# Decayed linear attention and token mixer on one core: decay moved to v and q, heads as array tiles, states by one scan, casts on GpSimd, mixer in four stages

## The chip, the cores and the metric

The kernel runs on one core of one Trainium2 chip. The metric is the device time of one execution in microseconds; before the change three runs gave 182.01 us as the median (181.44 to 183.78). Engines: PE is TensorE (matmul and transpose), DVE is VectorE, ACT is ScalarE, POOL is GpSimd, SP is SyncE, which here only issues transfers. Each engine runs its own instructions in the order in which they stand and waits for others by semaphores.

## The reference

Inputs: q, k, v of shape (4 batches, 8 heads, 768 tokens, 64), one decay lam per head, three weights. Cut to what matters:

```python
for b in range(nb):                                   # blocks of 64 tokens
    intra = einsum('bhic,bhjc->bhij', qb, kb) * Dmask # lam ** (i - j), lower triangle
    intra = einsum('bhij,bhjd->bhid', intra, vb)
    inter = einsum('bhid,bhde->bhie', qb * lam_pow, kv_state)
    out[:, :, sl] = intra + inter
    kv_state = lam_block * kv_state + einsum('bhsd,bhse->bhde', kb * rev_pow, vb)
x = out as (batch, token, 512)
wq, wk = x @ w_q, x @ w_k                             # 64 columns each
mixed = (wq @ wk.T / 8) @ x                           # over all tokens of a batch
result = relu(mixed) @ w_out
```

Both kernels use chunks of 128 tokens, write lam ** (i - j) as lam ** (i + 1) on the query side times lam ** -(j + 1) on the key side (counted from the start of the sequence), and compute mixed as wq (wk.T x), with Y = wk.T x.

## The kernel before, in words

A **pair** is two neighbouring heads of one batch (128 columns together); there are four pairs in a batch and 16 in all. The kernel goes through them in groups of two (`attention_pair`, L193), and after each second group comes the mixer of that batch (`hypermixer`, L296).

Set-up builds, for each pair number, three decay tables with Exp on ACT: dqT (lam ** t, transposed layout), dkT (not read later) and dkn (lam ** -t, natural layout), L131 to L142, and four padded query tiles `qTpad`, whose other half is zero (L62). `issue_dma` (L171) loads q and k from SP's queue and v from ACT's, one transfer of 192 KB for each head, one group ahead.

For each pair: ACT casts q (L199) and v (L201) to bf16, POOL multiplies k by dkn into khn (L203). PE transposes both (L208, L210); DVE multiplies the transposed q by dqT into two padded tiles (L212, L215), ACT copies the transposed k (L219). Then for each of six chunks: PE computes scores of both heads with all 128 rows of the array (L234; the zeros of qTpad take out the other head), DVE masks them (L242), PE multiplies with v into one half of the columns each (`ops`, L250), adds the state's part (L258), and forms this chunk's contribution to the state (`dps`, L268), which DVE adds to the running state gsb (L279). Every three chunks ACT copies `ops` into xT (L283).

The mixer of a batch: PE transposes xT back in 24 pieces (xnp, L302; DVE copies to xnat, L307), then wq (L313; ACT), wk (24 small matmuls, L326; DVE), Y (L338; DVE), `pm` (L351; ACT with relu into rmT) and the output product `po` (24 matmuls of 512 columns, L364; DVE copies to osb, L372; SP writes it out). All PSUM tiles rotate through one pool of eight banks, and osb through two buffers.

The program is written with a tile framework: a scheduler orders each engine's instructions from the dependencies, buffers and the order in which the code is written.

Of the kernel before, what the change touches and what calls it, by code (L numbers as in the profile page):

```python
# [10 lines left out]
BF16 = mybir.dt.bfloat16  # L12
# [5 lines left out]
BLK = 64  # L18
NB = S // BLK
# [10 lines left out]
def kernel(  # L30
# [14 lines left out]
    stage = ctx.enter_context(tc.tile_pool(name="stage", bufs=4))  # L45
    sbf = ctx.enter_context(tc.tile_pool(name="sbf", bufs=3))
    tsb = ctx.enter_context(tc.tile_pool(name="tsb", bufs=3))
    smk = ctx.enter_context(tc.tile_pool(name="smk", bufs=4))
    gsbp = ctx.enter_context(tc.tile_pool(name="gsb", bufs=4))
    xtp = ctx.enter_context(tc.tile_pool(name="xt", bufs=2))  # L50
    hyp = ctx.enter_context(tc.tile_pool(name="hyp", bufs=1))
    outp = ctx.enter_context(tc.tile_pool(name="outp", bufs=2))
    ps1 = ctx.enter_context(tc.tile_pool(name="ps1", bufs=8, space=bass.MemoryType.PSUM))
# [3 lines left out]
    qTpad = []  # L57
    for s_slot in range(2):
        pair = []
        for hl in range(2):  # L60
            qt = consts.tile([128, S], BF16, name=f"qTpad{s_slot}{hl}")
            nc.gpsimd.memset(qt[(1 - hl) * 64 : (1 - hl) * 64 + 64, :], 0.0)  # L62
            pair.append(qt)
        qTpad.append(pair)

    iota_i = consts.tile([128, 2, CH], F32, name="iota_i")
    nc.gpsimd.iota(
        iota_i,
        pattern=[[0, 2], [1, CH]],
        base=0,  # L70
        channel_multiplier=0,
        allow_small_or_imprecise_dtypes=True,
    )
    iota_p = consts.tile([128, 1], F32, name="iota_p")
    nc.gpsimd.iota(
        iota_p,
        pattern=[[0, 1]],
        base=0,
        channel_multiplier=1,
        allow_small_or_imprecise_dtypes=True,  # L80
    )
# [20 lines left out]
    EN4 = consts.tile([128, NCH, 2, D], F32, name="EN4")  # L102
    nc.gpsimd.iota(
        EN4,
        pattern=[[128, NCH], [0, 2], [0, D]],
# [3 lines left out]
    )  # L109

    lam_all = consts.tile([128, H], F32, name="lam_all")
    nc.sync.dma_start(out=lam_all, in_=lam.partition_broadcast(128))
    lnlam_all = consts.tile([128, H], F32, name="lnlam_all")
    nc.scalar.activation(out=lnlam_all, in_=lam_all, func=ACT.Ln)
    nlnlam_all = consts.tile([128, H], F32, name="nlnlam_all")
    nc.vector.tensor_scalar_mul(out=nlnlam_all, in0=lnlam_all, scalar1=-1.0)

    DqT = []
    DkT = []
    Dkn = []  # L120
    for kk in range(H // 2):
        lncol = consts.tile([128, 1], F32, name=f"lncol{kk}")
        nc.vector.tensor_copy(out=lncol[0:64, 0:1], in_=lnlam_all[0:64, 2 * kk : 2 * kk + 1])
        nc.vector.tensor_copy(
            out=lncol[64:128, 0:1], in_=lnlam_all[64:128, 2 * kk + 1 : 2 * kk + 2]
        )
        nlncol = consts.tile([128, 1], F32, name=f"nlncol{kk}")
        nc.vector.tensor_scalar_mul(out=nlncol, in0=lncol, scalar1=-1.0)
# [31 lines left out]
    def slot_col(hl, m, a):  # L160
        return (hl * 3 + (m - 6 * a) // 2) * BLK
# [261 lines left out]
```

## Time and profile before

| | |
|---|---|
| three runs, median | 182.01 us |
| span of the profiled execution | 179.5 us |
| PE busy | 120.8 us in 1272 matmuls |
| DVE busy | 98.8 us in 282 instructions |
| ACT busy | 79.0 us in 139 |
| POOL busy | 31.5 us in 30 |
| mean granted clock of PE | 0.903 of full speed |
| DMA | 26.7 MB, mean 149 GB/s |

A busy PE is not a PE at its peak: matmuls overlap, so a matmul's own time (about 0.26 us for 128 columns) is much longer than the distance to the next one. Times of a stage are therefore read from starts. [...]

### The profile page before, as it was taken

How to read it: one execution, taken by the hardware profiler on the slowest of the kernel's cores; microseconds unless marked ns; L12 is line 12 of the kernel's file. 1: busy time of each engine (PE TensorE's matmuls, PEld its weight loads, DVE VectorE, ACT ScalarE, POOL GpSimd, SP SyncE). 2: the span in 40 equal slices, each digit the busy share in tenths (PEclk: the TensorE clock that was granted, in tenths of full speed). 3: DMA queues.
4: the chain of work that ended last, by engine and by line, in shares of the span. 5: the costliest groups of instructions: out<-in, count | busy, mean ns of one | idle time of the engine just before them, and what ended most of it. 6: DMA issues, size and time to landing. Idle time of an engine off the chain costs nothing.

```text
span 179.5 us, 3380 instructions
## 1 busy us (share of the span) xinstructions
PE 120.8 (67%) x1272; PEld 73.6 (41%) x1272; DVE 98.8 (55%) x282; ACT 79.0 (44%) x139; POOL 31.5 (18%) x30
## 2 busy tenths in 40 slices
PE   0000038959969749779969679599697596896930
PEld 0000025636533426556534457375334374663310
DVE  0630018879532488677322896785327876972232
ACT  3019994665628501651534603926254016131600
POOL 8402520331600000606100005115000030000000
PEclk9999999999999985885899956969999759999995
DMA  3999949999997985497943650610005300000063
GB/s 84 328 285 282 270 108 262 285 260 240 237 225 158 295 243 167 102 257 172 219 91 104 201 177 4 147 28 4 0 4 220 128 4 2 4 0 4 0 234 117
DMA packets 80464, 26.70 MB, mean 149 GB/s; under 512 B 76864, under 2 KB 76864, under 8 KB 80448
## 3 DMA queue, kind: packets, MB, share of 16 engines
q1 hardware_dynamic: 55360, 20.20, 42.7%
q10 hardware_dynamic: 25088, 6.29, 15.5%
q8 instruction: 10, 0.16, 0.4%
q14 instruction: 6, 0.05, 0.1%
HBM read 20.19 MB, written 6.29 MB: 148 GB/s over the span
## 4 chain that ended last, share of the span: by engine, by line
PE 42%; issue 17%; DVE 14%; DMA 12%; ACT 11%; POOL 1%; ACTq 0%; DVEq 0%; POOLq 0%
PE po L364 7%; PE ops L250 7%; PE spsum L234 6%; DVE smask L242 5%; DMA out_dram<-osb 4%; PE xnp L302 4%; DMA vf<-in_v_dram 4%; DVE osb L372 3%; PE trq L208 3%; PE pq L313 3%; PE py L338 3%; PE pm L351 2%; PE ops L258 2%; ACT dkn L137 2%; DMA lam_all<-in_lam_dram 2%
## 5 line engine op out<-in xcount | busy, mean ns | idle before, releaser
L203 POOL TENSOR_TENSOR khn<-kf,dkn 128x768 bf16<-128x768 f32 x16 | 26.0, 1642 | 115.9 <-issue 78.2
L242 DVE TENSOR_TENSOR smask<-spsum,maskc 128x256 bf16<-128x256 f32 x96 | 36.5, 415 | 3.8 <-PE spsum L234 2.7
L234 PE MATMUL spsum<-qTpad,khatT 128*128 128x128 bf16 x192 | 25.6, 257 | 14.6 <-ACT khatT L219 7.5
L250 PE MATMUL ops<-smask,vn 128*64 128x128 bf16 x192 | 25.9, 265 | 5.5 <-DVE smask L242 5.2
L283 ACT CAST xT<-ops 128x384 bf16<-128x384 f32 x32 | 14.2, 481 | 34.7 <-PE ops L258 31.4
L372 DVE COPY osb<-po 128x512 f32<-128x512 f32 x24 | 16.0, 687 | 22.6 <-PE po L364 15.4
L208 PE MATMUL trq<-ident,qn 128*128 128x128 bf16 x96 | 11.2, 240 | 25.5 <-ACT qn L199 25.5
L364 PE MATMUL po<-wo_sb,rmT 128*128 128x512 bf16 x96 | 22.2, 380 | 0.0
L234 PEld LDWEIGHTS <-khatT 128*128 128x128 bf16 x192 | 13.5, 110 | 19.4 <-ACT khatT L219 13.8
L250 PEld LDWEIGHTS <-vn 128*64 128x64 bf16 x192 | 15.6, 121 | 14.1 <-issue 10.2
L212 DVE TENSOR_TENSOR qTpad<-trq,dqT 64x768 bf16<-64x768 bf16 x16 | 8.8, 549 | 22.5 <-PE trq L208 17.8
L258 PE MATMUL ops<-qTpad,gsb 128*64 128x128 bf16 x160 | 21.2, 260 | 0.0
L199 ACT CAST qn<-qf 128x768 bf16<-128x768 f32 x16 | 13.4, 838 | 15.1 <-PE trq L208 15.1
L358 ACT ACTIVATE rmT<-pm 128x512 bf16<-128x512 f32 (+1 forms) x32 | 12.7, 518 | 13.4 <-PE pm L351 13.4
L208 PEld LDWEIGHTS <-qn 128*128 128x128 bf16 x96 | 6.8, 106 | 28.2 <-ACT qn L199 25.8
L201 ACT CAST vn<-vf 128x768 bf16<-128x768 f32 x16 | 13.5, 842 | 8.1 <-PE ops L258 7.3
L268 PE MATMUL dps<-vn,khn 128*64 128x64 bf16 x160 | 16.6, 223 | 0.0
L219 ACT COPY khatT<-trk 128x768 bf16<-128x768 bf16 x16 | 12.5, 803 | 3.2 <-PE trk L210 3.1
L364 PEld LDWEIGHTS <-rmT 128*128 128x128 bf16 x96 | 8.2, 98 | 13.3 <-ACT rmT L358 5.7
L307 DVE COPY xnat<-xnp 128x512 bf16<-128x512 bf16 x24 | 8.9, 417 | 8.3 <-PE xnp L302 8.2
L279 DVE TENSOR_TENSOR gsb<-dps,gsb 128x64 bf16<-128x64 f32 x64 | 11.8, 215 | 2.4 <-PE dps L268 1.3
L258 PEld LDWEIGHTS <-gsb 128*64 128x64 bf16 x160 | 11.6, 129 | 2.7 <-issue 1.6
(44 smaller groups left out, 122.0 us busy)
## 6 DMA issues: line engine op xcount, KB each, us to landing
vf<-in_v_dram ACTq DMA_DIRECT2D x32, 192.0 KB, 4.4
qf<-in_q_dram SPq DMA_DIRECT2D x32, 192.0 KB, 4.0
kf<-in_k_dram SPq DMA_DIRECT2D x32, 192.0 KB, 3.9
out_dram<-osb SPq DMA_DIRECT2D x24, 256.0 KB, 2.1
wo_f<-in_moe_w_out_dram SPq DMA_DIRECT2D x1, 1024.0 KB, 7.2
wq_f<-in_moe_w_q_dram SPq DMA_DIRECT2D x1, 128.0 KB, 4.2
wk_f<-in_moe_w_k_dram SPq DMA_DIRECT2D x1, 128.0 KB, 4.9
lam_all<-in_lam_dram SPq DMA_DIRECT2D x1, 4.0 KB, 3.5
```

Of the source, the lines that this page charges most:

```text
L199: nc.scalar.copy(out=qn, in_=st.qf)
L201: nc.scalar.copy(out=vn, in_=st.vf)
L203: nc.gpsimd.tensor_tensor(out=khn, in0=st.kf, in1=Dkn[kk], op=ALU.mult)
L208: nc.tensor.transpose(trq[:, c * CH : (c + 1) * CH], qn[:, c, :, :], ident)
L234: nc.tensor.matmul(spsum[:, hl * CH : (hl + 1) * CH], L["khatT"][:, c * CH : (c + 1) * CH], L["qt"][hl][:, c * CH : (c + 1) * CH], start=True,
L242: nc.vector.tensor_tensor(out=smask, in0=spsum, in1=maskc, op=ALU.mult)
L250: nc.tensor.matmul(oreg, L["vn"][:, c, hl, :], Hh["smask"][:, hl * CH : (hl + 1) * CH], start=True, stop=(c == 0),)
L258: nc.tensor.matmul(oreg, gsb[:, :], L["qt"][hl][:, c * CH : (c + 1) * CH], start=False, stop=True,)
L268: nc.tensor.matmul(dps[hl * 64 : hl * 64 + 64, :], L["khn"][:, c, hl, :], L["vn"][:, c, hl, :], start=True, stop=True,)
L283: nc.scalar.copy(out=xT[st.b][:, st.kk, a * HALF : (a + 1) * HALF], in_=Hh["ops"],)
L364: nc.tensor.matmul(po, rmT[:, kt, stt * 128 : (stt + 1) * 128], wo_sb[:, kt, :], start=(kt == 0), stop=(kt == 3),)
L372: nc.vector.tensor_copy(out=osb, in_=po)
```

## The change

The attention part and the mixer are rewritten; loads, pools and order follow.

- **Loads**: one transfer of 384 KB for both heads of a pair, q, k and v all from SP's queue, two pairs ahead in the code, nine buffers for each; the weights come after pair 3.
- **Decay**: only on v (a small table DvI, 128 x 48, spread by broadcast) and on the transposed q (four tables Dq). k stays as it is.
- **Casts**: q and k are cast, and v is multiplied and cast, on POOL.
- **Heads as array tiles**: scores of a head use its 64 rows only (kT and qT slices at rows 0 or 64), with no padded tiles. The state's part uses 64 rows and 64 columns.
- **States by one scan**: all five chunk contributions of a pair are put into one PSUM tile, and one DVE scan with coefficients 0 and 1 makes the running sums for all chunks.
- **Masks** work on three chunks of a head at a time (128 x 384).
- **flip**: the transposes of xT back are done pair by pair, into one bank.
- **Mixer**: q and k projections in one matmul; wk by six transposes from that; Y and osb copied by ACT; a generator in four stages, of which one is run beside each pair of the next batch; the last batch's runs at the end.

```diff
-            nc.scalar.dma_start(
-                out=st.vf[:, :, hl, :],
+    def load(b, kk):
+        st = {}
+        for nm, src in (("q", q), ("k", k), ("v", v)):
+            t = stage.tile([128, 2, NCH, D], F32, tag="f" + nm, name="f" + nm)
+            nc.sync.dma_start(
+                out=t,
+                in_=src[b, 2 * kk : 2 * kk + 2].rearrange("h (c p) d -> p h c d", p=128),
+            )
...
+    staged = {0: load(*pairs[0]), 1: load(*pairs[1])}
...
-        dq = consts.tile([128, S], BF16, name=f"dqT{kk}")
-        nc.scalar.activation(out=dq, in_=ET, func=ACT.Exp, scale=lncol)
-        dk = consts.tile([128, S], BF16, name=f"dkT{kk}")
-        nc.scalar.activation(out=dk, in_=ET, func=ACT.Exp, scale=nlncol)
-        dkn = consts.tile([128, NCH, 2, D], BF16, name=f"dkn{kk}")
+    nc.scalar.preload_act_table_set("natural_log_exp_and_others")
...
+    DvI = consts.tile([128, H, NCH], F32, name="DvI")
+    nc.scalar.activation(out=DvI, in_=pw48, func=ACT.Exp, scale=-1.0)
...
+        nc.scalar.activation(out=t, in_=ET, func=ACT.Exp, scale=lncol[:, kk : kk + 1])
...
+    def prepare(n):
...
+        nc.gpsimd.tensor_copy(out=qn, in_=f["q"].rearrange("p h c d -> p c h d"))
+        kn = nat.tile([128, NCH, 2, D], BF16, tag="kn", name="kn")
+        nc.gpsimd.tensor_copy(out=kn, in_=f["k"].rearrange("p h c d -> p c h d"))
+        vn = nat.tile([128, 2, NCH, D], BF16, tag="vn", name="vn")
+        nc.gpsimd.tensor_tensor(
+            out=vn,
+            in0=f["v"],
+            in1=DvI[:, 2 * kk : 2 * kk + 2, :].unsqueeze(3).to_broadcast([128, 2, NCH, D]),
...
+            nc.tensor.transpose(trq[:, c * CH : (c + 1) * CH], qn[:, c, :, :], ident)
+        qT = tsb.tile([128, S], BF16, tag="qT", name="qT")
+        nc.vector.tensor_tensor(out=qT, in0=trq, in1=Dq[kk], op=ALU.mult)
...
+        nc.scalar.copy(out=kT, in_=trk)
+
+        dps = pst([128, D, NCH - 1], F32, "dps")
+        for c in range(NCH - 1):
+            for hl in range(2):
+                nc.tensor.matmul(
+                    dps[hl * 64 : hl * 64 + 64, :, c],
+                    kn[:, c, hl, :],
+                    vn[:, hl, c, :],
...
+        nc.vector.tensor_tensor_scan(
+            out=gs.rearrange("p e c -> p (e c)"),
+            data0=coef.rearrange("p e c -> p (e c)"),
+            data1=dps.rearrange("p e c -> p (e c)"),
...
+    def attend(n, L):
...
         for a in range(2):
...
+            sc = [pst([128, 3, CH], F32, f"sc{hl}") for hl in range(2)]
...
+                    r = slice(hl * 64, hl * 64 + 64)
+                    nc.tensor.matmul(
+                        sc[hl][:, cc, :],
+                        kT[r, c * CH : (c + 1) * CH],
+                        qT[r, c * CH : (c + 1) * CH],
...
+                    nc.tensor.matmul(
+                        oa[r, cc, :],
+                        gs[r, :, c - 1],
+                        qT[r, c * CH : (c + 1) * CH],
...
+                nc.vector.tensor_tensor(out=t, in0=sc[hl], in1=maskc, op=ALU.mult)
...
+                    nc.tensor.matmul(
+                        oa[r, cc, :],
+                        vn[:, hl, c, :],
+                        pr[hl][:, cc, :],
...
+            nc.scalar.copy(out=xT[b][:, kk, a * HALF : (a + 1) * HALF], in_=oa)
+
+    def flip(n):
...
+            nc.tensor.transpose(xp[:, t, :], xT[b][:, kk, t * CH : (t + 1) * CH], ident)
+        nc.vector.tensor_copy(out=xnat[b][:, :, kk * CH : (kk + 1) * CH], in_=xp)
...
+    def mixer(b):
...
+            nc.scalar.copy(out=qkT[:, n * HALF : (n + 1) * HALF], in_=pq)
...
+            nc.tensor.transpose(
+                pk[:, t, :], qkT[64:128, t * CH : (t + 1) * CH], ident[64:128, 64:128]
+            )
...
+        nc.scalar.copy(out=Y, in_=py)
+        yield
...
+        yield
...
+            nc.scalar.copy(out=osb, in_=po)
+            nc.sync.dma_start(out=out[b, t * CH : (t + 1) * CH, :], in_=osb)
+            if t % 3 == 2:
+                yield
...
+    ready = {0: prepare(0)}
+    mix = None
+    for n in range(N):
+        if n + 2 < N:
+            staged[n + 2] = load(*pairs[n + 2])
+        if n == 1:
+            load_weights()
+        if n + 1 < N:
+            ready[n + 1] = prepare(n + 1)
+        attend(n, ready.pop(n))
+        if n % NP == 0 and n > 0:
+            mix = mixer(n // NP - 1)
+        if mix is not None:
+            next(mix, None)
+        flip(n)
```

How the order of the instructions moves is seen at three places. The first is the start of the program on ACT. Before, with vf the v loads, dqT, dkT and dkn the tables:

```order
L186 DMA vf<-in_v_dram 128x6x64 x2
L114 ACT_TABLE_LOAD
L114 ACTIVATE lnlam_all<-lam_all 128x8 [waits DMAHW1_49]
L186 DMA vf<-in_v_dram 128x6x64 x3
L186 DMA vf<-in_v_dram 128x6x64 [waits DMAHW3_49]
L186 DMA vf<-in_v_dram 128x6x64 [waits DMAHW5_49]
L186 DMA vf<-in_v_dram 128x6x64 [waits DMAHW7_49]
L131 ACT_TABLE_LOAD [waits DVE_49]
L131 ACTIVATE dqT_121<-ET,lncol_116 128x768 [waits Pool_49]
L133 ACTIVATE dkT_123<-ET,nlncol_119 128x768 [waits DVE_49]
L137 ACTIVATE dkn_125<-EN_108,nlnlam_all 128x6x64 [waits Pool_49]
```

After:

```order
L105 ACT_TABLE_LOAD
L107 ACTIVATE lnl<-lam_all 128x8 [waits DMAHW0_49]
L126 ACTIVATE dq_124<-ET,lncol 128x768 [waits DVE_49,Pool_49]
L122 ACTIVATE DvI<-pw_120 128x48 [waits DVE_49]
L126 ACTIVATE dq_126<-ET,lncol 128x768
L126 ACTIVATE dq_128<-ET,lncol 128x768
L126 ACTIVATE dq_130<-ET,lncol 128x768
L176 COPY kT<-trk 128x768 [waits PE_49] x2
```

The six later v loads, of which three wait for a transfer, and the second table load are gone from between lnl and the first table; four tables and DvI stand ahead of the first copy of a transposed k.

The second place is DVE in the attention of the second batch. Before, a part of two pairs' chunks (smask the masked scores, gsb the running state, osb the output of the mixer before):

```order
L242 TENSOR_TENSOR smask_882<-spsum_879,maskc_104 128x256
L242 TENSOR_TENSOR smask_887<-spsum_884,maskc_104 128x256
L277 CAST gsb_894<-dps_891 128x64
L277 CAST gsb_901<-dps_898 128x64
L372 COPY osb_799<-po_794 128x512
L372 COPY osb_807<-po_802 128x512
L242 TENSOR_TENSOR smask_906<-spsum_903,maskc_104 128x256
L242 TENSOR_TENSOR smask_911<-spsum_908,maskc_104 128x256
L279 TENSOR_TENSOR gsb_920<-dps_917,gsb_894 128x64
L279 TENSOR_TENSOR gsb_929<-dps_926,gsb_901 128x64
```

After, one whole pair, beside the mixer's third or fourth stage (qT the decayed queries, gs all running states, pr the masked scores of a head's three chunks, xnat the flipped xT):

```order
L171 TENSOR_TENSOR qT_989<-trq_982,dq0_124 128x768
L190 SCALAR_TENSOR_TENSOR gs_1011<-coef_111,dps_1000 128x320
L240 TENSOR_TENSOR pr_1026<-sc0_1013,maskc_108 128x384
L240 TENSOR_TENSOR pr_1028<-sc1_1014,maskc_108 128x384
L240 TENSOR_TENSOR pr_1052<-sc0_1037,maskc_108 128x384
L240 TENSOR_TENSOR pr_1054<-sc1_1038,maskc_108 128x384
L261 COPY xnat_629<-xp_1087 128x6x128
```

A pair has seven DVE instructions, none of them the mixer's, where two pairs' chunks and osb copies alternated.

The third place is ACT beside the mixer's second stage. Before, after the mixer's relu (rmT) come the casts of the next pairs:

```order
L358 ACTIVATE rmT_737<-pm_753 128x256
L358 ACTIVATE rmT_737<-pm_756 128x512
L358 ACTIVATE rmT_737<-pm_759 128x256
L199 CAST qn_1057<-qf_811 128x768
L201 CAST vn_1059<-vf_813 128x768
L186 DMA vf_1429<-in_v_dram 128x6x64 x2
```

After, the eight rmT alternate with a pair's kT and xT:

```order
L176 COPY kT_747<-trk_740 128x768
L305 ACTIVATE rmT_812<-pm_813 128x384
L305 ACTIVATE rmT_812<-pm_816 128x384
L254 CAST xT_628<-oa_770 128x384
L305 ACTIVATE rmT_812<-pm_819 128x384
L305 ACTIVATE rmT_812<-pm_822 128x384
L254 CAST xT_628<-oa_794 128x384
L305 ACTIVATE rmT_812<-pm_825 128x384
L305 ACTIVATE rmT_812<-pm_828 128x384
L305 ACTIVATE rmT_812<-pm_831 128x384
L305 ACTIVATE rmT_812<-pm_834 128x384
L176 COPY kT_873<-trk_866 128x768
```

The relu of a batch now stands between the copies of the next batch's second pair; the last four come before the next kT.

## Rows read from the trace of the kernel before

**Rows 1.** The page: busy time (share, instructions); clock and GB/s by fortieths.

```profile
PE 120.8 (67%) x1272; PEld 73.6 (41%) x1272; DVE 98.8 (55%) x282; ACT 79.0 (44%) x139; POOL 31.5 (18%) x30
...
PEclk9999999999999985885899956969999759999995
...
GB/s 84 328 285 282 270 108 262 285 260 240 237 225 158 295 243 167 102 257 172 219 91 104 201 177 4 147 28 4 0 4 220 128 4 2 4 0 4 0 234 117
```

**Rows 2.** The chain that ended last, in order of time: start us, us, what.

```profile
4.66 7.47 DMA vf<-in_v_dram
...
25.49 0.82 PE trq L208 x6
...
44.79 0.33 PE xnp L302 x4
...
157.30 0.33 PE xnp L302 x4
...
175.25 0.69 DVE osb L372
```

**Rows 3.** PE in order of time: start us, us, line, tile, array shape, count.

```profile
40.40 0.40 PE L234 MATMUL spsum<-qTpad,khatT 128*128 128x128 bf16 x4
40.73 0.25 PE L268 MATMUL dps<-vn,khn 128*64 128x64 bf16 x4
40.91 0.40 PE L234 MATMUL spsum<-qTpad,khatT 128*128 128x128 bf16 x4
41.24 0.25 PE L250 MATMUL ops<-smask,vn 128*64 128x128 bf16 x2
...
41.53 0.25 PE L250 MATMUL ops<-smask,vn 128*64 128x128 bf16 x2
...
45.28 0.68 PE L302 MATMUL xnp<-ident,xT 128*128 128x128 bf16 x9
45.89 0.25 PE L250 MATMUL ops<-smask,vn 128*64 128x128 bf16 x2
...
50.58 1.48 PE L338 MATMUL py<-xnat,wkn 128*64 128x512 bf16 x6 [0.65 <-DVE wkn L333]
...
84.19 1.14 PE L302 MATMUL xnp<-ident,xT 128*128 128x128 bf16 x9
...
130.56 5.60 PE L364 MATMUL po<-wo_sb,rmT 128*128 128x512 bf16 x24
```

**Rows 4.** Groups by shape: line, engine, tile, count, busy us, mean ns, idle before.

```profile
L242 DVE TENSOR_TENSOR smask<-spsum,maskc 128x256 bf16<-128x256 f32 x96 | 36.5, 415 | 3.8 <-PE spsum L234 2.7
L203 POOL TENSOR_TENSOR khn<-kf,dkn 128x768 bf16<-128x768 f32 x16 | 26.0, 1642 | 115.9 <-issue 78.2 <-PE dps L268 17.3 <-ACT dkn L137 12.6
...
L283 ACT CAST xT<-ops 128x384 bf16<-128x384 f32 x32 | 14.2, 481 | 34.7 <-PE ops L258 31.4 <-DMA vf<-in_v_dram 3.1
...
L219 ACT COPY khatT<-trk 128x768 bf16<-128x768 bf16 x16 | 12.5, 803 | 3.2 <-PE trk L210 3.1
L279 DVE TENSOR_TENSOR gsb<-dps,gsb 128x64 bf16<-128x64 f32 x64 | 11.8, 215 | 2.4 <-PE dps L268 1.3
...
L358 ACT ACTIVATE rmT<-pm 128x512 bf16<-128x512 f32 x16 | 9.9, 620 | 13.4 <-PE pm L351 13.4
L215 DVE TENSOR_TENSOR qTpad<-trq,dqT 64x768 bf16<-64x768 bf16 x16 | 9.0, 561 | 0.5
L307 DVE COPY xnat<-xnp 128x512 bf16<-128x512 bf16 x24 | 8.9, 417 | 8.3 <-PE xnp L302 8.2
...
L95 POOL IOTA ET<- 128x768 f32 x1 | 0.8, 764 | 0.0
```

**Rows 5.** One stretch: us, busy time (count) of each engine, granted clock, DMA share, GB/s.

```profile
60.00:85.00 25.00, 18.43 (x226) 13.05 (x224) 19.51 (x58) 10.06 (x16) 5.69 (x4) 0.76 0.81 203
```

More of the change, by code (lines that the diff above doesn't have):

```diff
@@ L55 @@
+    pairs = [(b, kk) for b in range(B) for kk in range(NP)]
+    lam_all = consts.tile([128, H], F32, name="lam_all")
+    nc.sync.dma_start(out=lam_all, in_=lam.partition_broadcast(128))
+    staged = {0: load(*pairs[0]), 1: load(*pairs[1])}
     ident = consts.tile([128, 128], BF16, name="ident")
     make_identity(nc, ident)
[L57 to L64, printed above, removed]
@@ L109 @@
     )
[L111 to L123, printed above, removed]
+    maskc = consts.tile([128, 3, CH], BF16, name="maskc")
@@ L222, in attention_pair @@
+    def attend(n, L):
+        b, kk = pairs[n]
+        if b not in xT:
+            xT[b] = xtp.tile([128, NP, S], BF16, tag="xT", name="xT")
+            xnat[b] = xtp.tile([128, NCH, HD], BF16, tag="xnat", name="xnat")
+        qT, kT, vn, gs = L["qT"], L["kT"], L["vn"], L["gs"]
         for a in range(2):
-            half = {}
-            for st in streams:
-                ops = ps1.tile([128, HALF], F32, tag="p1", name="ops")
-                half[id(st)] = dict(ops=ops)
+            sc = [pst([128, 3, CH], F32, f"sc{hl}") for hl in range(2)]
@@ new lines, in attend @@
+            oa = pst([128, 3, CH], F32, "oa")
+            first = [True, True]
+            for cc in range(3):
+                c = 3 * a + cc
+                if c == 0:
+                    continue
+                for hl in range(2):
+                    r = slice(hl * 64, hl * 64 + 64)
+                    nc.tensor.matmul(
+                        oa[r, cc, :],
+                        gs[r, :, c - 1],
+                        qT[r, c * CH : (c + 1) * CH],
+                        start=first[hl],
+                        stop=False,
+                        skip_group_check=True,
+                    )
+                    first[hl] = False
@@ new lines, in attend @@
+            nc.scalar.copy(out=xT[b][:, kk, a * HALF : (a + 1) * HALF], in_=oa)
+    def flip(n):
+        b, kk = pairs[n]
+        xp = pst([128, NCH, CH], BF16, "xp")
+        for t in range(NCH):
+            nc.tensor.transpose(xp[:, t, :], xT[b][:, kk, t * CH : (t + 1) * CH], ident)
+        nc.vector.tensor_copy(out=xnat[b][:, :, kk * CH : (kk + 1) * CH], in_=xp)
+    def mixer(b):
+        xTb, xnb = xT[b], xnat[b]
+        wqk, wo = W["qk"], W["o"]
+        qkT = hyp.tile([128, S], BF16, tag="qkT", name="qkT")
+        for n in range(2):
+            pq = pst([128, HALF], F32, "pq")
+            for kt in range(NP):
@@ L337, in hypermixer @@
-        for tt in range(NCH):
-            nc.tensor.matmul(
-                py,
-                wkn[:, tt, :],
-                xnat[:, tt, :],
-                start=(tt == 0),
-                stop=(tt == NCH - 1),
-            )
-        nc.vector.tensor_copy(out=Ysb, in_=py)
+            nc.scalar.copy(out=qkT[:, n * HALF : (n + 1) * HALF], in_=pq)
+        pk = pst([128, NCH, DHY], BF16, "pk")
+        for t in range(NCH):
+            nc.tensor.transpose(
+                pk[:, t, :], qkT[64:128, t * CH : (t + 1) * CH], ident[64:128, 64:128]
+            )
@@ L351, in hypermixer @@
                 nc.tensor.matmul(
                     pm,
[L353 to L354 removed]
+                    Y[:, dd * CH : (dd + 1) * CH],
+                    qkT[0:64, n * HALF : (n + 1) * HALF],
                     start=True,
```

378 lines of the change are left out of this document (128 added, 250 removed).

## The prediction

> **What bounds the kernel now.** I read the page's busy shares first. No engine is full: DVE 98.8 us, ACT 79.0, POOL 31.5 of a span of 179.5 [rows 1], so the limit changes with the stage, and the chain of waits shows the stages [rows 2]. Up to 25.49 us TensorE does nothing. The chain goes through the v transfer that ACT's own queue issues (4.66, 7.47 us long); behind it ACT builds twelve Exp tables and only then casts the first q. From 25.49 to 44.79 run the first four pairs of heads, then the first mixer. The first transpose of the last mixer starts at 157.30, so one batch (four pairs, then a mixer) takes (157.30 - 44.79) / 3 = 37.5 us. From there to the end are 22.2 us. 25.5 + 19.3 + 3 x 37.5 + 22.2 = 179.5.
>
> Inside a batch two limits alternate. In the attention part it is DVE: per pair two qTpad of 0.56, six smask of 0.415 and five gsb of 0.215 [rows 4], 4.7 us, and between 60 and 85 us DVE is busy 19.5 of 25 us while the granted clock is 0.76 [rows 5]. In the mixer it is TensorE and its hand-overs, with DVE and ACT mostly waiting. The loads run beside this: 262 to 285 GB/s in the best early slices, under 150 in many of the later ones [rows 1]. The kernel does not wait for bandwidth after the start.
>
> **The change, part by part.**
>
> *Start, to the first attend with a mixer beside it.* The twelve Exp tables become four and a small one, one table load instead of two, and no load is issued from ACT's queue. The new PE order puts prepare(n+1) ahead of attend(n), so the first pairs follow the data. attend(4) needs pair 5: six pairs of 1.18 MB, and the weights (1.31 MB) that stand in SP's queue behind pair 3, 8.39 MB. The slices are 4.49 us long; the first five moved 84, 328, 285, 282 and 270 GB/s, 5.60 MB by 22.4 us [rows 1]. The other 2.79 MB at 270 take 10.3: landed at 32.8. Then the vn multiply, which is khn's operation on the same size (1.64, [rows 4]), and ten dps (0.45): **35 us**. At 285 GB/s it is 34, at 240 it is 36. The compute of pairs 0 to 3 lies below that: pair 1 has landed at 10.8 by the same slices, with vn and dps attend(0) starts at 13, and an iteration without a mixer is about 4.7 us (4.45 + 0.25 in the working below): 13 + 4 x 4.7 = 32.
>
> *POOL.* Per pair it now casts q and k and multiplies v. No cast on POOL is in the trace. The nearest rows are the iota of 128x768 f32 (0.76, one stream) and khn (1.64, two streams in) [rows 4]; I take 1.2. Per pair 4.0 us (3.2 to 4.9), with 4 us for the weights: 16 x 4.0 + 4 = 69 us, below the pace of the data (1.18 MB at 270 GB/s = 4.4 us) and of the batch below. It costs nothing as long as these hide it; at 1.64 the start is late by 5 us.
>
> *TensorE per pair.* Spacing, from start to start at full clock [rows 3]: transposes 0.068 (nine between 45.28 and 45.89), dps 0.045 (four between 40.73 and 40.91), column tiles in a mixture 0.048 (six between 41.24 and 41.53), spsum 0.082 (four in 0.33). After: 18 transposes 1.22 (a flip of six takes the place of the mixer's xnp), 10 dps 0.45, 22 inter and oa 1.06. The score matmuls on 64 rows are not in the trace: between 0.048, if two heads run side by side, and 0.082; at 0.067, 12 are 0.8. Together 3.5 us.
>
> *TensorE per mixer.* 512 columns take 0.233 (24 in 5.60, [rows 3]), so 384 take 0.175. pq 8 x 0.175 = 1.4, pk six transposes 0.3 (before: 24 matmuls), py 1.48, pm 1.4, po 5.6: 10.2. A batch is 4 x 3.5 + 10.2 = **24.2 us** of TensorE if it never waits.
>
> *DVE per pair.* qT 0.56 (one instead of two), four pr, xp copy and one scan. smask took 0.415 at 256 and gsb 0.215 at 64 columns: 1.04 ns a column, so pr at 384 is 0.55. The xp copy at 768 bf16 is 0.417 + 256 x 0.52 = 0.55 (xnat's row, at half the slope for bf16). The scan over 320 is not in the trace: by the slope 0.48; above, the five adds that it replaces, 1.07. I take 0.65. Sum 3.95 (before 4.7, and osb, Ysb besides). [...]
>
> *ACT.* Per pair kT 0.80 and two xT of 0.48: 1.76 [rows 4]. It takes over Y and osb (0.62 each by the 512-column row) and gives the q and v casts to POOL.
>
> *How these lie in one iteration* (pair n, beside one stage of the mixer of the batch before). PE issues trq, trk, dps: 1.27. The scan follows with a hand-over of 0.2 and ends at 2.1; the four pr end at 4.3, 4.45 with the hand-over. PE has scores, inter, po or pq to do until then. Stages 3 and 4 (three po groups each): six of the twelve po and the flip stand behind the last pr: 4.45 + 0.25 + 1.4 + 0.4 = 6.5. Stage 1: in the new order pk stands behind all oa and waits for ACT's qkT cast (0.48), py waits for DVE's wkn (about 0.4), nothing else stands between: 4.7 + 0.8 + 0.65 + 1.48 + 0.4 = 8.0. Stage 2: ACT has 1.76 + eight rmT at 0.48 = 5.6, and the next kT queues behind the last four: 6.2. **A batch is 8.0 + 6.2 + 6.5 + 6.5 = 27.2** instead of 37.5. The mixer's waits, 22.2 us at the end of the old kernel, are hidden below attention in three batches of four.
>
> *End.* The last mixer has no cover. pq 1.4, qkT 0.65, pk 0.3, wkn 0.6, py 1.5, Y 0.75, first four rmT 2.1, then po 5.6, osb 0.7: 13.6. The old kernel ended 3.6 after its last osb [rows 2]: 17.2. Four output buffers instead of two, so the osb no longer wait for the transfers.
>
> *Sum.* 35 + 3 x 27.2 - 2.5 (ten prepares in the loop, not twelve) + 17.2 = 131.3. The profiled execution of before is 2.5 under the median of the runs (182.0): **134**.
>
> **Rivals.**
>
> *PSUM banks.* A batch now takes 58 of eight rotating banks (10 per pair, 18 per mixer), before 84 (15 per pair, 24 per mixer). 37.5 us allow a mean hold of 3.6 us; the forecast needs 8 x 27.2 / 58 = 3.75 or less. An oa bank is opened by the inter matmuls and held through two pr and the xT. If the mean hold is 5 us, a batch is 36.3: 161. Against it: all four scores are released in 2.2 us of DVE.
>
> *Changes of array shape.* After, 223 neighbours in PE's order differ in rows or columns (before 178), and 135 of them have a 64-row shape on one side (before 8). In the old kernel the step from 128*64 to 128*128 costs nothing visible: four dps, then spsum after 0.18; the way back adds about 0.06 [rows 3]. Whether rows behave so, no row shows. If such a step waits until the array is empty, it costs a matmul's 0.25 less the spacing, 0.2: 27 us, a fifth of it under the wait for data: 156. [...]
>
> *POOL as the bound.* Above 2.6 us a cast, POOL passes 27.2 / 4 per pair. At twice khn (3.3) it is 8.2 per pair: last vn at 13 + 15 x 8.2 + 11 = 147, then 4.7 + 17.2 + 2.5: 171. For it: q and k are read in a permuted order, head by head. Against it: the runs stay 64 values long.
>
> [...]
>
> **How the numbers follow.** Forecast 0.68 (its own range 121 to 146: batches at 24.2 and everything at the lower bounds give 122; scores at 0.082, scan 1.07, casts at 1.64 and 1.5 us more waiting a batch give 146), banks 0.11 (161), shape changes 0.07 (156), POOL 0.08 (171), clock 0.04 (199); 0.02 is left for a wait not thought of. The range 121 to 158 holds the first, the third and half of the second. About 2% is what a measurement can tell from no change; faster 0.94, same 0.02, slower 0.04.
>
> **What would show it.** First matmul near 6 us, attend(4)'s scores at 33 to 37; pq of one batch to pq of the next 27 us apart; DVE near 65 us in all, ACT 70, POOL 60 to 80; casts 0.8 to 1.6; scans 0.5 to 0.8; from the last pq to the end 17. The forecast is wrong if scores wait for PSUM releases for more than 1 us in each iteration, if POOL is busy without a gap from start to end, if 64-row matmuls stand 0.2 apart at each change, or if the clock is below 0.8 after 40 us.

## The result, and the profile after

The changed kernel takes 156.4 us (median of four runs, 153.8 to 159.8), the kernel before 181.7 in the same comparison: a ratio of 0.852, 95% interval 0.842 to 0.861. The ratio is taken from the two faster runs of the changed kernel (153.8 and 155.2 us), while the profiled execution is one of the two others, so some 3 of the microseconds that follow are spread between runs. The forecast was 134.0 with the range 121 to 158. So the sign, the large gain and the range came true, and the time itself lies 22 us above the forecast. Most of what follows is on those 22 us. The profiled execution has a span of 155.9 us (157.7 with what lies around it), against a sum of 131.3 in the prediction: 24.6 to explain.

The page of the changed kernel, answering to [rows 1] (busy time; PEclk, which is the clock granted to TensorE in tenths of full speed, and GB/s by fortieths, now 3.9 us each):

```profile
PE 126.3 (81%) x1200; PEld 71.5 (46%) x1200; DVE 61.8 (40%) x121; ACT 64.7 (41%) x123; POOL 55.5 (36%) x61
...
PEclk9999999999999999999955699999957999999999
...
GB/s 72 222 222 219 218 219 240 293 206 220 209 218 214 226 76 0 69 202 234 307 232 202 228 153 4 81 252 256 279 203 226 24 0 0 169 105 135 0 189 214
```

DVE and ACT fell to about where they were expected (65 and 70 had been said); POOL rose to 55.5 us, less than the 60 to 80 that had been said. TensorE is busy 81% and all others 41% or less: it is the bound, where it does not wait. Two things are new. The early slices move 218 to 222 GB/s, not the 270 to 328 of [rows 1]. And the transfers stop twice in the middle (76, 0, 69 and 153, 4, 81), and each time the clock record falls 11 to 12 us after these slices (at 78.2 and 112.3 us).

The groups by shape, answering to [rows 4] (count, busy us, mean ns, idle before):

```profile
L240 DVE TENSOR_TENSOR pr<-sc,maskc 128x384 bf16<-128x384 f32 x64 | 30.8, 544 | 0.0
...
L161 POOL TENSOR_TENSOR vn<-fv,DvI 128x768 bf16<-128x768 f32 x16 | 23.5, 1472 | 19.7 <-DMA fv<-in_v_dram 14.3 <-PE oa L246 2.7 <-PE pk L281 2.0
...
L157 POOL CAST qn<-fq 128x768 bf16<-128x768 f32 x16 | 13.2, 823 | 32.2 <-DMA fq<-in_q_dram 31.8 <-PE trq L169 0.4
L190 DVE TENSOR_TENSOR_SCAN gs<-coef,dps 128x320 bf16<-128x320 f32 x16 | 13.1, 821 | 17.7 <-PE dps L181 17.4
...
L181 PE MATMUL dps<-vn,kn 128*64 128x64 bf16 x160 | 9.4, 286 | 8.3 <-POOL vn L161 8.2
```

Every duration is near its forecast (pr 544 ns for 0.55, the xp copy 555 for 0.55, the cast 823 between 0.76 and 1.64, the scan 821 between 0.48 and 1.07). What was not forecast stands in the last columns: POOL, and behind it TensorE, waited for transfers.

The chain that ended last, answering to [rows 2] (start us, us, what; each mixer begins with pq, and the dps ahead of it is of the pair prepared beside its first stage):

```profile
28.45 7.35 DMA fv<-in_v_dram
...
44.37 0.67 PE dps L181 x10
47.27 1.07 PE pq L271 x3
54.75 0.42 PE dps L181 x10
68.96 6.21 DMA fv<-in_v_dram
76.86 0.48 PE dps L181 x10
79.22 1.07 PE pq L271 x3
88.77 0.42 PE dps L181 x10
103.42 7.27 DMA fv<-in_v_dram
112.38 0.74 PE dps L181 x10
115.35 1.07 PE pq L271 x3
122.83 0.42 PE dps L181 x10
140.49 1.31 PE pq L271 x8
```

Read as the prediction's three terms: the scores behind the dps of 44.37 start at 45.0 (forecast 35: +10.0). From there to the last pq are 95.5 us (forecast 81.6 - 2.5 = 79.1: +16.4). From the last pq to the end are 15.4 (forecast 17.2: -1.8). Together +24.6. The loop's excess divides by the distances between dps:

| part of the loop | forecast | measured in the three batches | excess |
|---|---|---|---|
| stage 1 | 8.0 | 10.4, 11.9, 10.45 | +8.7 |
| stage 2 | 6.2 | 5.7, 5.7 | -1.0 |
| stage 3 | 6.5 | 7.0, 7.0 | +0.9 |
| stage 4, with the wait at its end | 6.5 | 9.4, 10.9 | +7.4 |
| stages 2 to 4 of the third batch, to the last pq | 16.7 | 17.7 | +1.0 |
| from dps (44.4) to scores (45.0), counted at the start | | | -0.6 |

The three transfers of v on the chain mark the slow start and the two waits in stage 4; behind each of them stands a slow stage 1. Stage 1 is slow at TensorE itself: three pq take 1.07 us, 0.36 each, in all three batches, but the eight of the last mixer take 1.31, 0.16 each. The granted clock is 0.57 and 0.68 in the second and third of these stages: the clock record of this run holds two levels, 1.00 and 0.50 of full speed, and reads 0.50 from 78.2 to 88.4 and from 112.3 to 119.1 us. So part of each ran at the lower level.

### The profile page after: what moved, and what is told of

Same layout as the page of the kernel before. It is cut to its first block, busy times and chain, and to the rows that moved or that the text cites. A ratio compares the mean times of both kernels' runs of the same rounds, so it can differ in the third digit from the quotient of the medians.

```text
span 155.9 us, 3005 instructions
## 1 busy us (share of the span) xinstructions
PE 126.3 (81%) x1200; PEld 71.5 (46%) x1200; DVE 61.8 (40%) x121; ACT 64.7 (41%) x123; POOL 55.5 (36%) x61
## 4 chain that ended last, share of the span: by engine, by line
PE 47%; SPq 19%; DMA 15%; DVE 6%; issue 5%; POOL 3%; ACT 3%; DVEq 0%; POOLq 0%; ACTq 0%
SPq L59 17%; DMA fv<-in_v_dram 13%; PE po L312 10%; PE oa L246 7%; PE pq L271 6%; PE py L288 5%; PE pm L298 4%; PE oa L228 4%; POOL vn L161 3%; PE xp L260 3%; PE dps L181 3%; DVE pr L240 2%; PE sc L212 2%; PE trq L169 2%; DMA out_dram<-osb 1%
## 5 line engine op out<-in xcount | busy, mean ns | idle before, releaser
L254 ACT CAST xT<-oa 128x384 bf16<-128x384 f32 x32 | 15.3, 479 | 45.9 <-PE oa L246 45.7
L240 DVE TENSOR_TENSOR pr<-sc,maskc 128x384 bf16<-128x384 f32 x64 | 30.8, 544 | 0.0
L161 POOL TENSOR_TENSOR vn<-fv,DvI 128x768 bf16<-128x768 f32 x16 | 23.5, 1472 | 19.7 <-DMA fv<-in_v_dram 14.3
L312 PE MATMUL po<-wo,rmT 128*128 128x512 bf16 x96 | 25.2, 382 | 0.0
L157 POOL CAST qn<-fq 128x768 bf16<-128x768 f32 x16 | 13.2, 823 | 32.2 <-DMA fq<-in_q_dram 31.8
L246 PE MATMUL oa<-pr,vn 128*64 128x128 bf16 x192 | 20.8, 263 | 1.3 <-DVE pr L240 1.3
L190 DVE TENSOR_TENSOR_SCAN gs<-coef,dps 128x320 bf16<-128x320 f32 x16 | 13.1, 821 | 17.7 <-PE dps L181 17.4
L228 PE MATMUL oa<-qT,gs 64*64 64x128 bf16 x160 | 18.6, 285 | 0.0
L159 POOL CAST kn<-fk 128x768 bf16<-128x768 f32 x16 | 13.2, 827 | 14.3 <-DMA fk<-in_k_dram 14.3
L169 PE MATMUL trq<-ident,qn 128*128 128x128 bf16 x96 | 10.9, 259 | 7.1 <-POOL qn L157 7.1
L305 ACT ACTIVATE rmT<-pm 128x384 bf16<-128x384 f32 x32 | 13.4, 510 | 5.4 <-PE pm L298 5.4
L320 ACT COPY osb<-po 128x512 f32<-128x512 f32 x24 | 14.0, 599 | 3.3 <-PE po L312 1.7
L260 PE MATMUL xp<-ident,xT 128*128 128x128 bf16 x96 | 10.9, 247 | 2.9 <-ACT xT L254 2.8
L174 PE MATMUL trk<-ident,kn 128*128 128x128 bf16 x96 | 10.2, 257 | 3.0 <-POOL kn L159 3.0
```

Source lines behind the costliest of these rows:

```text
L161: nc.gpsimd.tensor_tensor(out=vn, in0=f["v"], in1=DvI[:, 2 * kk : 2 * kk + 2, :].unsqueeze(3).to_broadcast([128, 2, NCH, D]), op=ALU.mult,)
L169: nc.tensor.transpose(trq[:, c * CH : (c + 1) * CH], qn[:, c, :, :], ident)
L228: nc.tensor.matmul(oa[r, cc, :], gs[r, :, c - 1], qT[r, c * CH : (c + 1) * CH], start=first[hl], stop=False, skip_group_check=True,)
L240: nc.vector.tensor_tensor(out=t, in0=sc[hl], in1=maskc, op=ALU.mult)
L246: nc.tensor.matmul(oa[r, cc, :], vn[:, hl, c, :], pr[hl][:, cc, :], start=False, stop=(cc == 2), skip_group_check=True,)
L254: nc.scalar.copy(out=xT[b][:, kk, a * HALF : (a + 1) * HALF], in_=oa)
```

## The experiments

**A. Which wait stops the loop?** SP's queue in the changed kernel, in order of time (start us, us until issued):

```profile
64.75 2.73 SPq L321 DMA_DIRECT2D out_dram<-osb  x3
67.57 0.42 SPq L59 DMA_DIRECT2D fq<-in_q_dram  x1
...
68.96 1.82 SPq L59 DMA_DIRECT2D fv<-in_v_dram  x1
```

and POOL and TensorE at the same pair (pair 9; in brackets the idle time before, and what ended it):

```profile
72.19 0.82 POOL L157 CAST qn<-fq 128x768 bf16<-128x768 f32 x1 [11.29 <-DMA fq<-in_q_dram]
...
75.33 1.47 POOL L161 TENSOR_TENSOR vn<-fv,DvI 128x768 bf16<-128x768 f32 x1 [0.86 <-DMA fv<-in_v_dram]
```

```profile
76.86 0.47 PE L181 MATMUL dps<-vn,kn 128*64 128x64 bf16 x10 [1.82 <-POOL vn L161]
```

The loads of pair 9 stand in the code behind the first three output stores, and SP waits at each store for ACT's osb:

```profile
SPq L321 <- ACT osb L320: 55.2, 20, 14.2
```

(us in total, times, longest). At pair 13 it repeats: dps waits 3.07 us at 112.38. The loads had free buffers (by the code, pair 9 takes those of pair 0), but could not be issued before 67.57. Theory: this order makes the gap, and the waiting TensorE then starts the next stage at its lower level. Two kernels take it away in different manners. The first issues loads four pairs ahead (the weights then come after pair 5):

```diff
-    staged = {0: load(*pairs[0]), 1: load(*pairs[1])}
+    staged = {m: load(*pairs[m]) for m in range(4)}
...
-        if n + 2 < N:
-            staged[n + 2] = load(*pairs[n + 2])
+        if n + 4 < N:
+            staged[n + 4] = load(*pairs[n + 4])
```

> The changed kernel with loads issued four pairs ahead in the code instead of two; nothing else. Theory (order on SP's queue): the loads of pairs 9 and 13 no longer stand behind output transfers that wait for osb, so the two gaps before their dps (about 2 and 4 us) go, and stage 1 of the mixer in the second and third batch, which ran at the low clock after these gaps, shortens from 11.9 and 10.4 to about 8.5 us: 10 to 13 us less than the changed kernel, 142 to 145 us. The weights now stand behind pair 5, so the scores of the fifth pair start near 40 instead of 45 us. Rival (the low clock in stage 1 comes from that stage's own waits for ACT and DVE): only the gaps go, 6 us, and stage 1 stays above 10 us at a low clock: 148 to 150 us.

Measured: 145.0 us, ratio 0.800 (0.795 to 0.805); both gaps are gone, and the pq of the four batches stand at 41.9, 73.2, 101.6 and 126.7. The first of them is 5.4 us earlier than in the changed kernel (the weights come later here), and from the first to the last it is 84.8 us instead of 93.2. The second leaves the loads alone and issues the stores from ACT's queue:

```diff
-            nc.sync.dma_start(out=out[b, t * CH : (t + 1) * CH, :], in_=osb)
+            nc.scalar.dma_start(out=out[b, t * CH : (t + 1) * CH, :], in_=osb)
```

> The changed kernel with the output transfers issued from ACT's queue, behind the osb copy that they wait for anyway; loads two pairs ahead and weights behind pair 3, as in the changed kernel. Theory (order on SP's queue): no load waits for an osb any more, so the gaps of 2 and 4 us before the dps of pairs 9 and 13 go, and stage 1 in the second and third batch runs at 8 to 9 us with its first three pq in 0.6 instead of 1.07 us; 9 to 12 us less than the changed kernel, 142 to 146, less or more by what 24 issues of 0.4 us on ACT cost. Rival (what four pairs ahead gained came from the weights that moved behind pair 5): gaps and low clock stay, 153 to 156 us.

Measured, in two runs: 146.3 us, ratio 0.805 (0.796 to 0.814). Its chain, the rows that answer to those above:

```profile
44.38 0.67 PE dps L181 x9
47.28 1.07 PE pq L271 x3
...
74.29 0.42 PE dps L181 x10
76.49 0.59 PE pq L271 x3
82.44 0.42 PE dps L181 x10
...
104.34 0.59 PE pq L271 x3
...
127.96 1.31 PE pq L271 x8
```

The start is the same to 0.01 us, both gaps are gone, and three pq now take 0.59 in the second and third batch. Stage 1 there is 8.15 us (74.29 to 82.44; forecast 8.0), and pq to pq is 27.85 (forecast 27.2; the distances on either side are 29.2 and 23.6). In the first batch, which still comes out of waits for data, pq takes 1.07 and stage 1 10.2. Both parts of the theory are shown: SP's order made the gaps, and without a gap the next stage ran at the upper level. It cost 11.5 of the 24.6 us by the two profiled spans (155.9 and 144.4), and 8.5 by the two ratios (0.852 and 0.805).

**B. Is it the v load alone?** The second kernel was meant for the start: v loads from ACT's queue, as before the change, so that two queues share the loads.

```diff
-            nc.sync.dma_start(
+            (nc.scalar if nm == "v" else nc.sync).dma_start(
```

> The changed kernel with the v loads issued from ACT's queue, as the old kernel did; size and shape of the transfers stay. Theory (one queue is slower than two): the early slices rise from about 220 GB/s to 270 or more, the scores of the fifth pair start near 37 instead of 45 us, and the time falls by about 6 to 8 us, less what ACT loses by standing in its queue while a load waits. Rival (the larger transfers in another shape are slower): the early slices stay at 220 GB/s and the time within 2 us of the changed kernel.

Measured: 151.6 us, ratio 0.834 (0.828 to 0.840). The early rate stayed at 217, so the second queue is not what the old start had. The first pq is even later, at 52.6. The gain came behind it: pq to pq is 31.6, 27.4 and 23.2 us (31.9, 36.1 and 25.1 in the changed kernel), where the v loads no longer stand behind the stores. That fits A, but the loads of q and k still stand there (SP waits 54.0 us at stores), and no run separates the two.

**C. Why do the loads run at 218 GB/s?** The kernels of this part go back to the old loads step by step: one transfer per head (192 KB), the old layout of the staging tile (chunk, then head), the tensors in turn, and all of it with v on ACT (the edit of this last one is shown, without the casts, which then read that layout).

```diff
-        for nm, src in (("q", q), ("k", k), ("v", v)):
-            t = stage.tile([128, 2, NCH, D], F32, tag="f" + nm, name="f" + nm)
-            nc.sync.dma_start(
-                out=t,
-                in_=src[b, 2 * kk : 2 * kk + 2].rearrange("h (c p) d -> p h c d", p=128),
-            )
-            st[nm] = t
+        for nm in ("q", "k", "v"):
+            st[nm] = stage.tile([128, NCH, 2, D], F32, tag="f" + nm, name="f" + nm)
+        for hl in range(2):
+            for nm, src in (("q", q), ("k", k), ("v", v)):
+                (nc.scalar if nm == "v" else nc.sync).dma_start(
+                    out=st[nm][:, :, hl, :],
+                    in_=src[b, 2 * kk + hl].rearrange("(c p) d -> p c d", p=128),
+                )
...
```

> The changed kernel with each load split into one transfer for each head (192 KB, the old shape), all from SP's queue. Theory (one queue is slower than two): the early slices stay near 220 GB/s, the time within 2 us of the changed kernel. Rival (size and shape): 270 GB/s or more, the scores of the fifth pair near 37 us, and 6 to 8 us less.

> The changed kernel with the staging tiles laid out as in the old kernel (chunk, then head, then 64 values: runs of 256 bytes that alternate between the heads of a partition) and one transfer of 192 KB for each head, all from SP's queue; everything after the staging as before. Theory (the layout that the load writes sets the rate, since neither a second queue nor 192 KB transfers changed it): the early slices rise from 218 to 250 GB/s or more, as in the old kernel with all loads on SP's queue (246 to 272), and the scores of the fifth pair start at 40 to 42 instead of 45 us: 3 to 5 us less than the changed kernel. Rival (the rate falls because more is running beside the loads, or because of the order of the loads): it stays at 218 and the time within 2 us.

> Loads four pairs ahead and the old staging layout together. If the layout sets the rate, the fifth pair's scores start near 35 us and the time is 3 to 5 us below that of four pairs ahead alone (145.0): 140 to 142. By the rival it is 144 to 146.

> The changed kernel with the old staging layout, one transfer for each head, all on SP's queue, and now in the old order: q, k, v of one head, then q, k, v of the other, so that neighbours in the queue read different tensors. Theory (neighbours that read one tensor's adjacent 192 KB lower the rate): the early slices rise from 218 to 250 GB/s or more, as in the old kernel with all loads on SP's queue, and the fifth pair's scores start at 40 to 42 us. Rival (something that runs beside the loads lowers it, or the number of loads waiting in the queues): 218 again.

> The changed kernel with the old kernel's loads in every respect: layout, one transfer for each head, q and k on SP's queue, v on ACT's, alternating tensors. If the transfers themselves set the rate, the early slices reach 270 or more; if what runs beside them does, they stay near 218 and only the order in the queues moves the time, as with v on ACT's queue (151.6 us).

A sixth kernel comes from the other side, the old kernel with its v loads on SP:

```diff
-            nc.scalar.dma_start(
+            nc.sync.dma_start(
```

> The old kernel with the v loads issued from SP's queue instead of ACT's. If ACT's queue held up the start, the second table load starts near 5 instead of 12.7 us and the first matmul at about 17 to 19 instead of 25.5 us. By the theory that one queue is slower, its early slices fall to about 220 GB/s; by the rival they stay at 270 to 285. Time: 175 to 181 us where the later loads are still in time.

Measured, with the rate between 8 and 20 us of each kernel:

| kernel | time, us | ratio to before | GB/s |
|---|---|---|---|
| changed kernel | 156.4 | 0.852 | 220 |
| one transfer per head | 154.2, two runs | 0.849 (0.844 to 0.855) | 218 |
| per head, old layout | 153.8, two runs | 0.85 | 217 |
| the same, four pairs ahead | 145.6 | 0.801 (0.791 to 0.811) | 218 |
| per head, old layout, tensors in turn | 158.8, one run | 0.88 | 218 |
| old loads in all, v on ACT | 154.0, one run | 0.85 | 214 |
| old kernel, v on SP | 173.4, two runs | 0.955 (0.948 to 0.962) | 243 (209, 254, 268 by thirds) |
| old kernel | 181.7 | 1 | 281 |

None of these theories of the rate holds: with the old loads in the new kernel it stays at 214 to 218. The old kernel with v on SP is faster by 4.5%: the transfers there no longer delay ACT (its second table load moves from 12.66 to 7.01 us, the first transposes from 25.5 to 19.8), so a part of the change's gain at the start is that line alone.

**D. Casts.** One part of the change undone, though not to the letter: the casts of q and k go to ACT (the old kernel had those of q and v there), POOL keeps the product for v. It also tells whether POOL's work beside the loads slows them.

```diff
-        nc.gpsimd.tensor_copy(out=qn, in_=f["q"].rearrange("p h c d -> p c h d"))
+        nc.scalar.copy(out=qn, in_=f["q"].rearrange("p h c d -> p c h d"))
...
-        nc.gpsimd.tensor_copy(out=kn, in_=f["k"].rearrange("p h c d -> p c h d"))
+        nc.scalar.copy(out=kn, in_=f["k"].rearrange("p h c d -> p c h d"))
```

> The changed kernel with the casts of q and k on ACT, as the old kernel had q's, and only the v multiplication on POOL: one part of the change undone. Theory on the rate (POOL's casts beside the loads lower it): the early slices rise from 218 to 250 GB/s or more. Rival: 218 as before. On the time: ACT gains 32 casts of 0.83, 27 us, and is at 91 of some 155 us; the casts stand in ACT's order behind xT and rmT, so stage 2 of the mixer becomes longer by 1.7 us a batch and the time rises by 3 to 8 us if ACT decides there, and by less than 2 us if the loads' pace covers it.

Measured, in two runs: 176.3 us, ratio 0.974 (0.963 to 0.985), rate 218. POOL's casts do not set the rate. But the casts on ACT cost 20 us, far more than the 3 to 8 expected: most of what the change had gained. In its chain:

```profile
140.12 2.31 ACT rmT L305 x6
142.43 0.72 ACT kn L159
143.19 0.82 PE trk L174 x6
144.01 0.67 PE dps L181 x7
```

ACT is busy 88.4 us instead of 64.7, still only half the span. The cast stands in ACT's queue behind six relu of the mixer, the transposes of the next pair wait for the cast, and dps at 0.67 instead of 0.42 shows that TensorE then runs at its lower level (the clock record of this kernel is 0.72 to 0.74 from 100 to 160 us). TensorE's transposes wait 18.8 us in all for these casts, 10.1 for POOL's in the changed kernel; how the rest divides between the lower level and other waits was not measured. So the order of the change needs the casts on POOL, though the prediction gave that move no price of its own.

**E. Where the tiles lie.** What was left was not in the transfers' code at all. By the addresses in the built programs, which no trace shows, the first staging tile of the changed program starts at byte 44064 of each partition, 32 past a multiple of 256, because the constants ahead of it have other sizes. In the kernel before it starts at 65792, which is 257 x 256. The tiles are 3072 bytes, so all share this offset, and each packet is 256 bytes (64 values; 2.64 MB in 10412 packets from 8 to 20 us in the changed kernel). A tile of 224 bytes ahead of all others restores the boundary:

```diff
+    pad = consts.tile([128, 56], F32, name="pad")
+    nc.vector.memset(pad, 0.0)
     lam_all = consts.tile([128, H], F32, name="lam_all")
```

> One tile of 224 bytes per partition stands ahead of all others, so that every staging tile starts at a multiple of 256 bytes, as in the kernel before (in the changed kernel they start 32 bytes past one). Everything else is as in the changed kernel. Theory that the start address of the destination sets the rate of the 256-byte packets: the plateau of the first 24 us rises from 218 to 250 to 288 GB/s, the scores of attend(4) start at 37 to 40 us instead of 45, the loads behind the two gaps land about 1.2 us sooner each, and the time is 146 to 151 us. Rival, that the rate comes from the engines that work beside the loads: the plateau stays at 218 and the time at 155 to 158.

> The same pad tile together with loads that run four pairs ahead. If the address sets the rate, the first batch, which is paced by its data in the kernel with loads four ahead (pq of the first batch at 41.9 us, 145.0 us in all), comes 4 to 6 us earlier and the time is 138 to 141 us, with no gap left. If the rate stays at 218, 145 us.

The stretch from 8 to 20 us of the kernel before, of the changed kernel and of the padded one (busy time and count of PE, PEld, DVE, ACT and POOL; clock, DMA share, GB/s), and what the DMA view says of the same stretch:

```profile
8.00:20.00 12.00, 0.00 (x0) 0.00 (x0) 2.29 (x7) 7.33 (x10) 2.17 (x2) 1.00 1.22 281
```

```profile
8.00:20.00 12.00, 6.64 (x67) 4.51 (x67) 4.39 (x8) 2.08 (x4) 6.82 (x7) 1.00 1.27 220
...
q1 hardware_dynamic: 10412, 2.64, 127.0%
```

```profile
8.00:20.00 12.00, 8.23 (x83) 5.46 (x81) 4.33 (x8) 2.68 (x5) 8.49 (x8) 1.00 1.16 263
...
q1 hardware_dynamic: 12447, 3.15, 115.6%
```

The share counts 16 engines, so a packet takes 1.27 x 12 x 16 / 10412 = 23.4 ns in the changed kernel and 1.156 x 192 / 12447 = 17.8 ns in the padded one. (Shares above 100% mean that the recorded times of packets overlap; so the rate rises only by 263 / 220 = 1.20.) In the old kernel it is 18.3 (1.221 x 192 / 12841 packets), and 17.9 with v on SP. In all ten kernels whose staging tiles start 32 bytes past the multiple, a packet takes 23.4 to 25.5 ns at 214 to 220 GB/s; in the four that start on it, 17.8 to 18.3 at 243 to 281. The pad moves the other tiles behind it too, but the engines' times stay: pr 543 ns, casts 825, scan 821 in the padded kernel, as in the changed one. The start address of the destination is the cause of the slow packets. Whether a smaller boundary than 256 would do was not tried, and why the old kernel's 281 lies above the 263 at an equal time per packet is open (it had two queues).

The time: 149.6 us with the pad alone (156.4 without it), 141.2 with the pad and four pairs ahead (145.0 without it). The four runs of each lie apart (144.6 to 152.1, and 138.8 to 144.0), so no interval was made; against a median of 181.6 the ratios are 0.82 and 0.78. That the first batch with four pairs ahead would come 4 to 6 us earlier was missed: its pq stands at 40.4 for 41.9, and most of the gain lies behind it (27.85 to the next pq, for 31.4). The second one is the best version of this study. The chain of its profiled execution (137.0 us):

```profile
13.99 0.75 PE dps L183 x10
...
38.24 0.42 PE dps L183 x10
40.44 0.59 PE pq L273 x3
46.39 0.42 PE dps L183 x10
...
121.56 1.31 PE pq L273 x8
```

No DMA row delays it after the start, stage 1 is 8.15 us (38.24 to 46.39, and the same in the other batches), and the tail is 15.4 as in the changed kernel. In the version with the pad alone both gaps remain (dps waits 1.47 and 2.63 us for vn), and its first three pq take 1.07 behind each of them: the pad moves the start, SP's order the loop.

## Why the prediction was right, and where it missed

The sign was right, and 25 of the 48 us forecast came, for the reason given: the mixer's waits went below attention, and the loop and the end came out as summed wherever TensorE did not wait for a load. That the range held 156.4 is partly luck: it lies outside the forecast's own 121 to 146, and the stated range reached to 158 for the sake of rivals that did not make this time.

*Start, 35 us forecast, 45.0 measured.* The step that failed is the load rate, "the other 2.79 MB at 270". It took the old kernel's rate over to another program. The cost of the error follows from the bytes: 8.39 MB at 218 instead of 270 GB/s are 7.4 us more. The case was on its own list at "240 it is 36", but that applied the lower rate to the last 2.79 MB only. The v of pair 5 was forecast to have landed at 32.8; POOL takes it as soon as it lands, in the changed kernel and in the padded one:

```profile
41.82 1.47 POOL L161 TENSOR_TENSOR vn<-fv,DvI 128x768 bf16<-128x768 f32 x1 [1.70 <-DMA fv<-in_v_dram]
```

```profile
36.22 1.47 POOL L163 TENSOR_TENSOR vn<-fv,DvI 128x768 bf16<-128x768 f32 x1 [1.72 <-DMA fv<-in_v_dram]
```

```profile
39.42 0.70 PE dps L183 x9
```

The rate is thus worth 5.6 us of landing. The dps of this pair moves by 5.0, from 44.37 to 39.42 in the padded kernel (last row), and no further, since the other path then decides: "13 + 4 x 4.7 = 32" took iterations at the upper clock level. In the padded kernel four pairs ahead, where dps goes from 13.99 to 38.24 in four pairs with no transfer on the chain, one takes 6.1 us. TensorE changes between its levels there: ten dps take 0.75 in the first of these places and 0.42 in the last, and the granted clock is 1.00 from 20 to 24 us, 0.58 from 24 to 28 and 0.93 from 28 to 32.

Even with the rate restored the scores start near 40 (padded kernel), or near 39 with the weights later, not at 35.

The packets of the runs without the pad and with it differ by 23.4 / 17.8 = 1.31 in time. The sizes of the tiles ahead of the destination could have been summed up before the run, but no row of the kernel before showed that they matter; the run with the pad does.

*Loop, 79.1 forecast, 95.5 measured.* The sum of work per batch came out: 27.85 between pq in the kernel with stores on ACT, for 27.2, and stage 1 at 8.15 for 8.0. The step that failed is "The kernel does not wait for bandwidth after the start", said of the kernel before and carried over, together with the sentence on four output buffers: the prediction counted the stores at the tail alone, and never walked SP's queue to see what stands behind a store that waits for ACT. Loads on SP were priced by bytes, not by when they can be issued. SP waits 55.2 us at stores, and dps waited 1.82 and 3.07 us for the late loads of pairs 9 and 13. This cost twice, as longer stages 4 (7.4 us in all) and as a slower stage 1 behind each (11.9 and 10.45 us for 8.15).

*Tail, 17.2 forecast, 15.4 measured.* Right to 1.8 us.

*Operations.* The scan is 0.82, above the 0.65 taken and between the prediction's 0.48 and 1.07. It made no time here, as DVE is not the bound. The half slope taken for bf16 is what the two copies give: 417 ns at 512 columns before (xnat) and 555 at 768 now (xp) are 0.54 ns a column, where f32 had 1.04. POOL's cast is 0.82 for 1.2, and vn 1.47 for 1.64, so POOL is not the bound.

*The rivals.* Banks: PE waits 1.3 us in all at oa, for pr, and no score waits for a bank. POOL as the bound is refuted by its 55.5 us. The 199 us stood for TensorE at a lower clock through loop and end; no run shows that term. In its place the runs show the lower level in the start and in each stage behind a wait, about 2.4 to 3.9 us a batch.

Shape changes are real, at about half the rival's price. A stretch of PE in the changed kernel at the upper level:

```profile
66.33 0.50 PE L260 MATMUL xp<-ident,xT 128*128 128x128 bf16 x6
66.67 0.50 PE L169 MATMUL trq<-ident,qn 128*128 128x128 bf16 x6
67.00 0.50 PE L174 MATMUL trk<-ident,kn 128*128 128x128 bf16 x6
67.43 0.47 PE L181 MATMUL dps<-vn,kn 128*64 128x64 bf16 x10
67.83 0.34 PE L212 MATMUL sc<-qT,kT 64*128 64x128 bf16 x6
68.11 0.36 PE L228 MATMUL oa<-qT,gs 64*64 64x128 bf16 x4
```

Six transposes take 0.34 and 0.33 us where the next group has the same shape, though tiles and weights change, and 0.43 where dps follows: the change costs 0.10. In the single starts it is the same throughout: 0.056 from one transpose to the next, 0.149 from trk to dps in each of the four places from 54.8 to 76.8 and from 89 to 112 us. Six scores need 0.28, but they come in twos, one of each head, that start 0.004 apart, and the next two 0.06 later; the rest is the step to the inter matmuls, again about 0.1. The prediction's reading that a step "costs nothing visible" does not hold; its spacings of 0.068 and 0.082 had a step in them (0.056 within the groups, 0.149 behind their last). So its sum had a change at nothing that takes 0.1, and a score at 0.067 that takes 0.03. The two missed on opposite sides, and that the stages without a wait came out near the forecast is partly luck. What TensorE does in the 0.10 us of a change no run tells. That 156.4 agrees with the price of the shape-change rival (156) is chance: the 24.6 us are found in the start and behind the waits for loads.

## What to carry to other kernels

Walk the queue that issues the loads, not only its bytes: a store that waits for an engine holds back every load behind it, and a few loads more in front, or another queue for the stores, removed 8 to 11 of 156 us here. Before taking over a transfer rate, sum the sizes of the tiles ahead of the destination: 32 bytes beside a 256-byte boundary made each 256-byte packet 1.31 times as long, and the rate 218 to 220 GB/s for 263. And where an engine is half empty, ask whose queue an instruction stands in: casts that fit ACT's idle time by the sum cost 20 us behind its relu. Where TensorE is the bound, put matmuls of one shape together: the 223 changes of shape that the prediction counts are, at 0.1 us each, some 22 us of TensorE (an estimate; no run tried it).

## What the runs showed of the hardware that was not expected

- The start address in SBUF changes the time of a 256-byte packet: 23.4 ns against 17.8, with 220 and 263 GB/s from the same loads.
- A change of the array's shape between neighbouring matmuls costs about 0.1 us at the upper clock level (six transposes 0.43 us instead of 0.33), and two 64-row scores on different rows start 0.004 us apart.
- The clock record read 1.00 up to its first fall (at 78.2 us in the changed kernel, 66.1 in the kernel before), also where matmuls took the times of the lower level: in the kernel with stores on ACT both stretches below read 1.00, while three pq take 1.07 us in the first and 0.59 in the second.

```profile
44.40:54.60 10.20, 9.66 (x86) 4.95 (x88) 3.67 (x8) 3.15 (x6) 6.03 (x6) 1.00 1.18 220
74.30:82.40 8.10, 7.40 (x84) 4.27 (x85) 3.99 (x9) 3.10 (x6) 3.12 (x3) 1.00 1.16 264
```

So the spacing of matmuls of one shape tells the level more surely than the column.
- A wait of TensorE of 1.5 to 3.1 us for one pair was followed by a stage of the mixer in part or wholly at the lower level (its first three pq in 1.07 or 1.08 us for 0.59), in each of the four places in the changed and in the padded kernel; in the changed kernel the granted clock over these stages is 0.57 and 0.68.
